# Row maxima of an attention kernel: four a unit as a + relu(b - a), single banks, and a table of paired slots

## The chip, the cores and the metric

The kernel runs on one core of a Trainium2 chip. The metric is device time of one execution in microseconds (us); the median of three runs before the change is 5821.26 us (5820.58 to 5821.32). Engine names are those of the profile: PE is TensorE's matmuls and PEld its weight loads, DVE is VectorE, ACT is ScalarE, POOL is GpSimd, SP is the engine from whose queue the DMAs are issued. PSUM, where matmuls write, has eight banks of 512 float32 columns on 128 partitions.

## The reference

Four transformer layers without MLP: A, B, A, B. A is multi-head attention with its own keys and values per head, B has 32 heads of queries and one shared head of keys and values. All is float32; S = 2048 positions, D = 576, H = 32 heads of 18.

```python
def _A_ref(x, wqkv, wo):
    qkv = (x @ wqkv).reshape(B, S, 3, H, Dh).transpose(2, 0, 3, 1, 4)
    q, k, v = qkv[0], qkv[1], qkv[2]
    scores = jnp.einsum("bhqd,bhkd->bhqk", q, k) * (Dh ** -0.5)
    p = _softmax(scores, axis=-1)
    o = jnp.einsum("bhqk,bhkd->bhqd", p, v)
    return o.transpose(0, 2, 1, 3).reshape(B, S, D) @ wo
# _B_ref is the same with k = x @ wk, v = x @ wv shared by all heads
x = A_x
x = x + _A_ref(_layernorm(x), A_wqkv, A_wo)
x = x + _B_ref(_layernorm(x), B_wq, B_wk, B_wv, B_wo)
# and both once more
```

## The kernel before

Queries and keys are projected, split into a high and a low part so that 54 rows (18 dimensions, three products) carry the precision, and stored to DRAM (`qk_d`); per pair of heads they are loaded back into `big`, head 0 on partitions 0 to 63 and head 1 on 64 to 127. The order of all work is written out by hand: the schedule is manual, each engine's instructions stand in the order in which the program makes them, and a tile waits for its buffer's last user.

The attention loop goes over units. A **unit** is one pair of heads (`p`, 16 of them) and one quarter of the queries (`u`, 512 of them); a layer has 64. A unit has

- 32 score matmuls for the **maxima** (`max_mm`, tile `psm`): for each of two heads `a`, four blocks of 128 queries `qc` and four blocks of 512 keys `kb`, queries on the partitions. DVE takes the maximum of each row of keys (`reduce_max`). `max_final` reduces the four key blocks of each query block to one negated maximum; POOL splits it into two parts, `max_store` transposes it and sends it to DRAM, `max_rows` loads it as two more rows of the query operand. The maxima of a unit are made `LEAD` steps (a step is four exponentials) ahead of its exponentials;
- 32 score matmuls for the **exponentials** (`exp_mm`, tile `pse`): keys on the partitions, 512 queries, with the two rows of the negated maximum in the product; ACT takes `exp` into a tile `pt` of the pool with 15 buffers;
- the **values** (`pv_block`): the `pt` tiles times the values, with a column of ones for the sum, accumulated in the one bank `oacc`: four tiles at a time on four column groups. `pv_cols` issues them as a run of so many columns, 4096 a unit. At the unit's end ACT copies `oacc` out (`oc`), and POOL and DMAs do the division.

A score matmul uses half of PE's rows (54 to 64 of 128), head 0 the upper, head 1 the lower half, so two of different heads can run side by side. The loop goes through `ORDERS`, eleven phases a unit: five of two maxima and three exponentials, five of four and three, one of two and two; after each phase a run of 384 columns of values (256 after the last), two phases behind. In `max_mm` two maxima share a tile of two banks (`mtile2`), and one `reduce_max` of 1024 elements does both.

PSUM before: two tiles of two banks for maxima (tag `m`), three single ones for exponentials (tag `e`), and `oacc`. The tags also serve the projections (`project`, `project_v`, `out_w`), which run between the loops with matmuls of all 128 rows; the first `2 * LEAD` pairs of maxima of a layer are woven between the last projections (`woven`, `beat`, `max_pair`).

```python
for phase in range(11 * 4 * NPAIR):
    k = phase % 11
    run_todo(LEAD + exps // 4)
    for kind, n in ORDERS[2 if k == 10 else k % 2]:
        ...
    exps += 2 if k == 10 else 3
    if phase >= 2:
        pv_cols(256 if k == 10 else 384)
```

## Time and profile before

| | |
|---|---|
| runs | 5821.32, 5821.26, 5820.58 us |
| profiled execution: span, first to last instruction | 5815.8 us; what lies around it is not in the profile (the runs' median is 5.5 us longer) |
| PE busy | 5782.9 us (99%), granted clock 0.998 |
| DVE busy | 5174.9 us (89%), of it 4773.0 in 4096 reductions of 1024 |
| ACT busy | 4604.8 us (79%), of it 4314.2 in 8192 exponentials |
| POOL busy | 1722.0 us (30%) |
| HBM | 45 GB/s over the span |

A group's row gives line, engine, operation, output and input tiles, shapes and count, then the busy time in us and the mean duration of one in ns, then the engine's idle time just before them and what ended it. Neighbouring operations of an engine overlap at their ends, so the distance from start to start is shorter than the duration. A row of the timeline gives start and length in us of a stretch of equal instructions, with their count; matmul rows of neighbouring stretches overlap. A row of a stretch (`A:B`) gives its length, then the busy time and count of PE, PEld, DVE, ACT and POOL, the granted clock, the share of the DMA engines and GB/s.

### The profile page before, as it was taken

To read this page: it belongs to the slowest core of one execution; us is meant where nothing else is said; L and a number is where in the kernel's file an instruction comes from. 1 tells how busy PE (TensorE), PEld (TensorE's weight loads), DVE (VectorE), ACT (ScalarE), POOL (GpSimd) and SP (SyncE) were. 2 spreads that over 40 slices of the span, in tenths; PEclk is the share of its full clock that TensorE was granted. 3 is DMA by queue.
4 is the path that set the end of the run, shared out by engine and by line. 5 is a ranking of instruction groups with operands and counts; after the bars stand their busy time and mean duration, and the time that the engine had idled before them with its cause. 6 is when DMAs were issued, how large, how long until landed. Compare 5 with 4: busy or idle time off the path is not lost.

```text
span 5815.8 us, 132694 instructions
## 1 busy us (share of the span) xinstructions
PE 5782.9 (99%) x53756; PEld 2904.4 (50%) x53756; DVE 5174.9 (89%) x5333; ACT 4604.8 (79%) x8872; POOL 1722.0 (30%) x2210
## 2 busy tenths in 40 slices
PE   8999999999999999999999999999999999999999
PEld 7644444444844444444685444444448444444446
DVE  4699999998699999999647999999976999999995
ACT  2488888888378888888625888888882888888885
POOL 2142323233233232323311323232342332323232
PEclk9999999999999999999999999999999999999999
DMA  5311111110320000001242111111114100000002
GB/s 194 111 42 35 32 35 32 35 32 21 126 65 23 23 20 22 20 23 23 59 167 87 44 35 31 35 31 35 29 32 129 51 22 23 22 23 19 23 14 77
DMA packets 250305, 276.40 MB, mean 48 GB/s; under 512 B 131732, under 2 KB 171924, under 8 KB 239972
## 3 DMA queue, kind: packets, MB, share of 16 engines
q1 hardware_dynamic: 249692, 267.92, 16.6%
q8 instruction: 422, 6.91, 0.5%
q14 instruction: 191, 1.56, 0.1%
HBM read 151.24 MB, written 112.56 MB: 45 GB/s over the span
## 4 chain that ended last, share of the span: by engine, by line
PE 97%; DVE 1%; POOL 0%; ACT 0%; DMA 0%; issue 0%; SPq 0%; POOLq 0%; ACTq 0%; DVEq 0%
PE oacc L683 36%; PE psm L509 31%; PE pse L658 17%; PE psn L219 6%; PE psq L377 6%; DVE mx L518 1%; PE ps L211 0%; ACT pt L662 0%; DMA raw<-in_B_wk_dram 0%; DMA raw<-in_A_wqkv_dram 0%; SPq L153 0%; POOL wsm L168 0%; PE oacc L212 0%; DVE big L168 0%; POOL big L168 0%
## 5 line engine op out<-in xcount | busy, mean ns | idle before, releaser
L518 DVE TENSOR_REDUCE mx<-psm 128x2 f32<-128x1024 f32 x4096 | 4773.0, 1217 | 171.9 <-PE psm L509 131.4
L662 ACT ACTIVATE pt<-pse 128x512 f32<-128x512 f32 x8192 | 4314.2, 602 | 543.5 <-PE pse L658 374.0
L658 PE MATMUL pse<-big 64*128 64x512 f32 x8192 | 2448.8, 417 | 3.5 <-ACT evr L388 1.8
L509 PE MATMUL psm<-big 62*128 62x512 f32 x8192 | 2295.4, 453 | 7.0 <-DVE mx L518 6.7
L683 PE MATMUL oacc<-pt,vbuf 128*19 128x384 f32 (+1 forms) x24560 | 1757.5, 385 | 1.9 <-ACT oc L689 1.9
L509 PEld LDWEIGHTS psm<-big 62*128 62x128 f32 x8192 | 926.3, 184 | 1480.9 <-DVE mx L518 926.7
L658 PEld LDWEIGHTS pse<-big 64*128 64x128 f32 x8192 | 1188.4, 185 | 286.1 <-ACT pt L662 193.6
L683 PEld LDWEIGHTS oacc<-pt,vbuf 128*19 128x19 f32 x24560 | 500.8, 97 | 772.9 <-issue 595.2
L141 POOL TENSOR_SCALAR hl<-neg 128x8 fp32r<-128x8 f32 x256 | 50.9, 199 | 2670.5 <-DVE neg L634 2670.5
L706 POOL TENSOR_TENSOR rl<-lt,mone 128x8 f32<-128x8 f32 x256 | 423.7, 1655 | 568.5 <-DMA lt<-os 568.2
L683 PE MATMUL oacc<-pt,vy 128*19 128x256 f32 x8176 | 591.5, 384 | 0.0
L141 POOL TENSOR_SCALAR os<-oc 32x512 f32<-32x512 f32 x512 | 314.6, 614 | 130.5 <-ACT oc L689 88.7
L719 POOL TENSOR_TENSOR os<-os,rb 96x512 f32<-96x512 f32 x256 | 329.5, 1287 | 21.3 <-DMA rb<-r_d 21.3
L697 POOL TENSOR_TENSOR os<-os,oc 96x512 f32<-96x512 f32 x256 | 326.6, 1276 | 21.4
L385 ACT ACTIVATE ev<-psq 128x512 fp32r<-128x512 f32 (+1 forms) x112 | 67.0, 598 | 335.4 <-PE psq L377 225.4
L219 PE MATMUL psn<-wsm,xx 128*128 128x288 f32 x2240 | 313.3, 297 | 0.0
L219 PEld LDWEIGHTS psn<-wsm,xx 128*128 128x128 f32 x2240 | 299.3, 188 | 15.9 <-issue 15.6
L683 PEld LDWEIGHTS oacc<-pt,vy 128*19 128x19 f32 x8176 | 176.8, 98 | 249.4 <-issue 200.3
L391 DVE TENSOR_TENSOR ev<-psq,ev 128x512 fp32r<-128x512 f32 (+1 forms) x84 | 58.0, 691 | 217.9 <-ACT ev L385 202.6
L377 PE MATMUL psq<-yx,big 128*128 128x512 f32 (+2 forms) x812 | 201.7, 399 | 7.7 <-DVE ev L391 4.8
L377 PE MATMUL psq<-xx,big 128*128 128x512 f32 (+1 forms) x784 | 201.0, 401 | 0.0
L689 ACT ACTIVATE oc<-oacc 128x512 f32<-128x512 f32 x256 | 157.7, 616 | 28.9 <-PE oacc L683 28.9
(70 smaller groups left out, 1372.3 us busy)
## 6 DMA issues: line engine op xcount, KB each, us to landing
big<-qk_d SPq DMA_DIRECT2D x180, 432.0 KB
qk_d<-ev SPq DMA_DIRECT2D x96, 512.0 KB
qk_d<-ev SPq DMA_DIRECT2D x120, 256.0 KB
rb<-r_d SPq DMA_DIRECT2D x512, 36.0 KB
o_d<-os SPq DMA_DIRECT2D x512, 36.0 KB
m_d<-tr SPq DMA_DIRECT2D x1024, 2.0 KB
o<-o_d SPq DMA_DIRECT2D x64, 256.0 KB
big<-m_d SPq DMA_DIRECT2D x512, 4.0 KB
```

The costliest lines, as they stand in the source:

```text
L141: eng.tensor_scalar(dst, src, 1.0, 0.0, op0=OP.mult, op1=OP.add)
L219: nc.tensor.matmul(ps, lhs[:, xc, :], wsm[:, wc, h * 288:(h + 1) * 288], start=i == 0, stop=i == len(TERMS) - 1)
L377: nc.tensor.matmul(ps[:n].rearrange("p (u t) -> p u t", u=2)[:, us], w[:, wc, :n], xts[T][:, us, xc, :], start=(xc, wc) == TERMS[0], stop= ...
L509: nc.tensor.matmul(ps[:, slot], q[b:b + KM, c0:c0 + P], k[b:b + KM, kb * 512:(kb + 1) * 512], start=True, stop=True)
L518: nc.vector.reduce_max(mxs[p, u][:, r0:r1 + 1:r1 - r0], ps, axis=AX.X)
L658: nc.tensor.matmul(e, k[r:r + KE, kc * P:(kc + 1) * P], q[r:r + KE, u * 512:(u + 1) * 512], start=True, stop=True)
L662: nc.scalar.activation(pt, e, AF.Exp, scale=SCALE)
L683: nc.tensor.matmul(oacc[j:j + DH + 1, cs], v_of(kc)[:, 2 * p + a if is_a else 0, :], pts[p, u, i][:, cs], start=kc < 2 and c0 == 0, stop=k ...
L689: nc.scalar.activation(oc, oacc, AF.Copy)
L697: nc.gpsimd.tensor_tensor(t[:96], t[:96], oc[:96], op=OP.add)
L706: nc.gpsimd.tensor_tensor(rl, lts.pop((p, u)), mone, op=OP.pow)
L719: nc.gpsimd.tensor_tensor(t[:96], t[:96], rb[:96], op=OP.mult)
```

## The change

1. **Maxima in pairs of key blocks.** For each head, two of the four query blocks of a unit have their first two key blocks done another way (four in all a unit, two per head): a matmul with the difference of the two key blocks (`d`, tile `psd`) gives b - a, ACT writes relu(b - a) to a tile `r`, and later the matmul of block 0 (`t`) gives a, and one DVE operation adds `r` and takes the maximum over the row: max(a, b) = a + relu(b - a). The other 24 maxima of a unit (`m`) have one `reduce_max` of 512 each. The first three units of a layer (`FIRST_SHARED`) have plain maxima only. The fused DVE operation is built as two instructions, the operation and a read of its accumulator.
2. **Key differences.** `key_diff` makes them while keys are projected (ACT keeps block 0's result, DVE subtracts, POOL splits), stores them to `kd_d`; `load_kd` loads them per pair of heads into the spare buffer `xx[:, 0]`, two DMAs each.
3. **The order.** `UNIT` replaces `ORDERS`: 32 slots a unit, each with one matmul of head 0 and one of head 1 (e exponential, m, d, t maxima), and twelve numbers that issue runs of values, 896 columns behind (`LAG`) instead of two phases. Units without maxima use `LAST`: eight times two slots of exponentials and 512 columns.
4. **Banks.** Three single tiles for maxima (`m` and `t`), four for exponentials and `d`, and `oacc`. The projections that used both banks of a double tile take one of each tag and are drained in halves.
5. **Lead.** `LEAD` is 16 steps instead of 14: 32 pairs of maxima ahead of the loop instead of 28.

In the built program ACT has 8871 activations before and 9875 after and 644 and 1950 separate waits; DVE 4352 and 6496 reductions, 384 and 460 two-input operations, and 976 fused ones with as many accumulator reads after; POOL gets 24 operations more, SP's queue 92 DMAs more. There is one load of ACT's table in both.

```diff
-LEAD = 14
+LEAD = 16
...
+UNIT = """ee md 384 me me em 512 dm md em 320 me ee em 192 em me 384 et ee mm 384 me ee em 384 dm me em 384
+          em me 256 me te ee 256 em em 384 et te me 256"""
+LAST = "ee ee 512 " * 8
+LAG = 896
...
+def max_ops(kinds):
+    pairs = kinds.count("d")
+    rest = [(qc, kb) for qc in range(4) for kb in range(4) if qc >= pairs or kb > 1]
+    seen, ops = {"d": 0, "t": 0}, []
+    for k in kinds:
+        if k == "m":
+            ops.append((k, *rest.pop(0)))
+        else:
+            ops.append((k, seen[k], 0))
+            seen[k] += 1
...
+FIRST_SHARED = 3
...
-    def mtile2(name):
-        return psum.tile([P, 2, 512], F32, tag="m", bufs=2, name=name)
-
     def mtile(name):
-        return mtile2(name)[:, 0]
+        return psum.tile([P, 512], F32, tag="m", bufs=3, name=name)
 
     def etile(name):
-        return psum.tile([P, 512], F32, tag="e", bufs=3, name=name)
+        return psum.tile([P, 512], F32, tag="e", bufs=4, name=name)
...
-        ps = mtile2("psn")
         for h in range(2):
-            natural(ot, h, ps[:, h])
-        xc = xo[:, c, :].rearrange("p (h n) -> p h n", h=2)
-        nc.vector.tensor_tensor(xc, ps[:, :, :288], xc, op=OP.add)
+            ps = natural(ot, h, (etile if h else mtile)("psn"))
+            xc = xo[:, c, h * 288:(h + 1) * 288]
+            nc.vector.tensor_tensor(xc, ps, xc, op=OP.add)
...
+        def key_diff(T, t, ps, r0, r1):
+
+            if T == 0:
+                k0s[t] = ptile("k0")
+                nc.scalar.activation(k0s[t][r0:r1], ps[r0:r1], AF.Copy)
+                return
+            kd, lo, hi = k0s.pop(t), ptile("kl"), ptile("kh", dt=F32R)
+            nc.vector.tensor_tensor(kd[r0:r1], ps[r0:r1], kd[r0:r1], op=OP.subtract)
+            copy(nc.gpsimd, hi[r0:r1], kd[r0:r1])
+            hi_f = hi.bitcast(F32)[r0:r1]
+            nc.gpsimd.tensor_tensor(lo[r0:r1], kd[r0:r1], hi_f, op=OP.subtract)
...
+            if kind == "d":
+                ps = etile("psd")
+                nc.tensor.matmul(ps, q[b:b + 3 * DH, c0:c0 + P], kds[p % 2 if is_a else 0][b:b + 3 * DH],
+                                 start=True, stop=True)
+                r = ptile("r")
+                diffs[a].append(r)
+                nc.scalar.activation(r, ps, AF.Relu)
+            else:
+                ps = tile("psm")
+                nc.tensor.matmul(ps, q[b:b + KM, c0:c0 + P], k[b:b + KM, kb * 512:(kb + 1) * 512],
+                                 start=True, stop=True)
+                if kind == "t":
+                    r = diffs[a].pop(0)
+                    nc.vector.tensor_tensor_reduce(out=r, in0=ps, in1=r, scale=1.0, scalar=-3.0e38, op0=OP.add,
+                                                   op1=OP.max, accum_out=mx[:, r0:r0 + 1])
+                else:
+                    nc.vector.reduce_max(mx[:, r0:r0 + 1], ps, axis=AX.X)
...
-                    woven(max_pair, 10, 5)
+                    woven(max_pair, 12, 4)
...
+            if is_a or p == 0:
+                at(max(LEAD + 32 * (p - 2) + 20, LEAD + 1 + p), load_kd, p)
...
+        late, n_e = LAG, 0
+        for w in range(4 * NPAIR):
+            p, u = divmod(w, 4)
+            more_m = m_done[0] < 4 * ns
+            e_next = [0, 0]
+            for kinds, cols in UNIT if more_m else LAST:
+                run_todo(LEAD + STEPS * w + sum(e_next) // 4)
+                for a in range(2):
+                    if kinds[a] == "e":
+                        n = e_next[a]
+                        e_next[a] += 1
+                        exp_mm(p, u, n // 2 * 4 + 2 * a + n % 2, mtile if not more_m and n_e % 7 % 2 else etile)
+                        n_e += 1
+                    else:
+                        max_mm(a, mtile)
+                skip = min(late, cols)
+                late -= skip
+                pv_cols(cols - skip)
```

More of the change, by code (lines that the diff above doesn't have):

```diff
@@ L59, with slots @@
 TAIL = 2
-ORDERS = ([("m", 1), ("e", 0), ("m", 1), ("e", 1), ("e", 2)],
-          [("m", 0), ("m", 1), ("e", 1), ("e", 0), ("m", 0), ("m", 1), ("e", 2)],
-          [("m", 1), ("e", 0), ("m", 1), ("e", 1)])
+UNIT = """ee md 384 me me em 512 dm md em 320 me ee em 192 em me 384 et ee mm 384 me ee em 384 dm me em 384
+          em me 256 me te ee 256 em em 384 et te me 256"""
+LAST = "ee ee 512 " * 8
+LAG = 896
+def slots(text):
+    out = []
+    for w in text.split():
+        if w.isdigit():
+            out[-1][1] = int(w)
+        else:
+            out.append([w, 0])
+    return out
+UNIT, LAST = slots(UNIT), slots(LAST)
+KINDS = [[w[a] for w, _ in UNIT if w[a] != "e"] for a in range(2)]
+assert sum(n for _, n in UNIT) == 4096 and [len(k) for k in KINDS] == [16, 16]
+def max_ops(kinds):
[8 more added lines that the diff above has]
+            seen[k] += 1
+    assert not rest
+    return ops
+MAX_OPS = [max_ops(k) for k in KINDS]
+PLAIN = [(i // 2 % 4, i // 8 % 2 * 2 + i % 2) for i in range(16)]
+FIRST_SHARED = 3
 @with_exitstack
@@ L114, in tile_kernel @@
     r_d = dram.tile([H, S], F32, name="r_d")
+    kd_d = dram.tile([D, 3, 512], F32, name="kd_d")
     rb = cst.tile([P, 512], F32, name="rb")
+    mxd = [cst.tile([P, 32], F32, name=f"mxd{i}") for i in range(2)]
+    for t in mxd:
+        nc.gpsimd.memset(t, -3.0e38)
+    kds = [xx[:, 0].rearrange("p c t -> p (c t)")[:, 512 * i:512 * i + 512] for i in range(2)]
     sums = [cst.tile([P, 512], F32, name=f"os{i}") for i in range(2)]
@@ L385, in project @@
             nc.scalar.activation(ev[0][:n], ps[:n], AF.Copy)
+            r0, r1 = ((64, P) if t == 4 else (0, P)) if is_a else (96, 96 + DH)
+            if T < 2 and t in (range(4, 9) if is_a else (4,)):
+                key_diff(T, t, ps, r0, r1)
             if filler:
@@ L402, in project, with load_kd @@
                 store(ev_f, 0, P, t * P, t0)
+        def key_diff(T, t, ps, r0, r1):
[8 more added lines that the diff above has]
+            nc.gpsimd.tensor_tensor(lo[r0:r1], kd[r0:r1], hi_f, op=OP.subtract)
+            c0 = t * P + r0 - D if is_a else 0
+            dst = kd_d[c0:c0 + r1 - r0]
+            nc.sync.dma_start(dst[:, 0:2], hi_f[:, None, :].to_broadcast([r1 - r0, 2, 512]))
+            nc.sync.dma_start(dst[:, 2], lo[r0:r1])
+        k0s = {}
+        def load_kd(p):
+            for a in range(2):
+                c = (2 * p + a) * DH if is_a else 0
+                nc.sync.dma_start(kds[p % 2 if is_a else 0].bitcast(F32)[64 * a:64 * a + 3 * DH],
+                                  kd_d[c:c + DH].rearrange("c i t -> (c i) t"))
         def store(ev_f, r0, r1, c0, t0):
@@ L424, in project_v @@
         def project_v(c):
-            ps = mtile2("psn")
-            for h in range(2):
-                natural(xt_of(c), h, ps[:, h])
-            return ps[:, :, :288].rearrange("p h (e d) -> p h e d", d=DH)
+            return [natural(xt_of(c), h, (etile if h else mtile)("psn")).rearrange("p (e d) -> p e d", d=DH)
+                    for h in range(2)]
         def v_dst(c):
@@ L484, in ops @@
             return big[:, q_slot(p)], big[:, k_slot(p)]
-        m_open, m_next, m_done, m_count = [], [0, 0], [0], {}
+        diffs, m_next, m_done, m_count = ([], []), [0, 0], [0], {}
         m_first = [] if is_a else ([(0, i // 2, i % 2) for i in range(8)] + [(1, i // 2, i % 2) for i in range(4)] +
@@ L491, in tile_kernel, with max_mm @@
                                    [(1, i, 2) for i in range(4)] + [(1, i, 3) for i in range(4)])
-        def max_mm(a, slot):
-            i = m_next[a]
-            p, u = divmod(i // 16, 4)
-            if i < len(m_first):
-                u, qc, kb = m_first[i]
-            else:
-                qc, kb = i // 2 % 4, i // 8 % 2 * 2 + i % 2
+        def max_mm(a, tile):
+            n = m_next[a]
+            w, i = divmod(n, 16)
+            shared = w >= FIRST_SHARED
+            kind = "m"
+            if n < len(m_first):
+                w, qc, kb = m_first[n]
+            elif shared:
+                kind, qc, kb = MAX_OPS[a][i]
+            else:
+                qc, kb = PLAIN[i]
+            p, u = divmod(w, 4)
@@ L501, in max_mm @@
             q, k = ops(p)
             if (p, u) not in mxs:
-                mxs[p, u] = pool.tile([P, 32], F32, name="mx")
-            if m_done[0] % 2 == 0:
-                m_open.append((mtile2("psm"), []))
-            ps, rows = m_open[0]
+                mxs[p, u] = mxd[w % 2] if shared else pool.tile([P, 32], F32, name="mx")
+            mx = mxs[p, u]
             b = 64 * a
             c0 = u * 512 + qc * P
-            nc.tensor.matmul(ps[:, slot], q[b:b + KM, c0:c0 + P], k[b:b + KM, kb * 512:(kb + 1) * 512],
-                             start=True, stop=True)
@@ L511, in max_mm @@
-            rows.append((p, u, 16 * a + 4 * qc + kb))
+            r0 = 16 * a + 4 * qc + kb
             m_next[a] += 1
             m_done[0] += 1
-            if m_done[0] % 2 == 0:
-                m_open.pop()
-                (p, u, r0), (p1, u1, r1) = sorted(rows)
-                assert (p, u) == (p1, u1)
-                nc.vector.reduce_max(mxs[p, u][:, r0:r1 + 1:r1 - r0], ps, axis=AX.X)
-                m_count[p, u] = m_count.get((p, u), 0) + 2
-                if m_count[p, u] == 32:
-                    max_final(p, u)
+            if kind == "d":
[15 more added lines that the diff above has]
+                    nc.vector.reduce_max(mx[:, r0:r0 + 1], ps, axis=AX.X)
@@ L523, in max_pair @@
+            m_count[p, u] = m_count.get((p, u), 0) + 1
+            if m_count[p, u] == 32:
+                max_final(p, u)
         def max_pair():
@@ L526, in max_pair @@
             for a in range(2):
-                max_mm(a, a)
+                max_mm(a, etile if a else mtile)
             if not is_a and m_done[0] == 46:
@@ L576, in last_values @@
                     staged.append((c, h, ptile("vst", (P, 16, DH))))
-                    nc.scalar.activation(staged[-1][2], pv[:, h], AF.Copy)
+                    nc.scalar.activation(staged[-1][2], pv[h], AF.Copy)
             vs.append(pool.tile([P, NV], F32, tag="vy", bufs=1, name="vy")
@@ L594, in tile_kernel @@
                 if not is_a and T == 2 and i == 1:
-                    woven(max_pair, 10, 5)
+                    woven(max_pair, 12, 4)
                 elif not is_a and T == 3:
-                    woven(max_pair, *((2, 7), (4, 3), (4, 3))[i])
+                    woven(max_pair, *((3, 4), (4, 3), (4, 3))[i])
                 project(T, t, not is_a and T >= 2)
@@ L618, in tile_kernel @@
                 for c in range(4 * T, 4 * T + 4):
-                    nc.scalar.activation(v_dst(c), project_v(c), AF.Copy)
+                    for h, ps in enumerate(project_v(c)):
+                        nc.scalar.activation(v_dst(c)[:, h], ps, AF.Copy)
         fill = []
@@ L650, in max_rows, with exp_mm @@
                                   m_d[u][:, a].rearrange("j q p -> j (q p)"))
-        def exp_mm(p, u, i, tail):
+        def exp_mm(p, u, i, tile):
             a, kc = (i // 2) % 2, i // 4 * 2 + i % 2
             q, k = ops(p)
-            e = (mtile if tail and i % 2 else etile)("pse")
+            e = tile("pse")
             r = 64 * a
@@ L742, in tile_kernel @@
                 for i in range(4 if is_a else 2):
-                    at(LEAD + 32 * (p - 1) + 1 + 8 * i if p else LEAD + 1 + 4 * i, load_part, p + 1, i)
+                    at(LEAD + 32 * (p - 1) + 1 + 8 * i if p else LEAD + 1 + 3 * i, load_part, p + 1, i)
+            if is_a or p == 0:
+                at(max(LEAD + 32 * (p - 2) + 20, LEAD + 1 + p), load_kd, p)
         for c in range(5):
@@ L768, in tile_kernel @@
         assert not weave["left"]
-        exps = 0
-        for phase in range(11 * 4 * NPAIR):
-            k = phase % 11
-            run_todo(LEAD + exps // 4)
-            for kind, n in ORDERS[2 if k == 10 else k % 2]:
-                if kind == "e":
-                    n += exps
-                    exp_mm(*divmod(n // 4 // STEPS, 4), n % (4 * STEPS), m_done[0] >= 4 * ns)
-                elif m_done[0] < 4 * ns:
-                    max_mm(n ^ k // 2 % 2, m_done[0] % 2 if k % 2 == 0 else n ^ k // 2 % 2)
-            exps += 2 if k == 10 else 3
-            if phase >= 2:
-                pv_cols(256 if k == 10 else 384)
+        late, n_e = LAG, 0
+        for w in range(4 * NPAIR):
+            p, u = divmod(w, 4)
+            more_m = m_done[0] < 4 * ns
+            e_next = [0, 0]
+            for kinds, cols in UNIT if more_m else LAST:
+                run_todo(LEAD + STEPS * w + sum(e_next) // 4)
+                for a in range(2):
+                    if kinds[a] == "e":
[3 more added lines that the diff above has]
+                        n_e += 1
+                    else:
+                        max_mm(a, mtile)
+                skip = min(late, cols)
+                late -= skip
+                pv_cols(cols - skip)
+            assert e_next == [16, 16]
+        assert not diffs[0] and not diffs[1]
         outs = out_proj(layer == 3)
@@ L786, in tile_kernel @@
                 next(outs)
-                pv_cols(256 * (1 + st - ns))
+                pv_cols(LAG - 512 if st == ns else 512)
         tail = [todo.pop(n, []) for n in range(ns + LEAD + L_AT + 1, ns + LEAD + O_AT)]
```

## The prediction

> **What bounds the kernel now.** I read the page first: its span, the busy shares, the granted clock, the chain of waits and the costliest groups.

> ```profile
> span 5815.8 us, 132694 instructions
> ...
> PE 5782.9 (99%) x53756; PEld 2904.4 (50%) x53756; DVE 5174.9 (89%) x5333; ACT 4604.8 (79%) x8872; POOL 1722.0 (30%) x2210
> ...
> PEclk9999999999999999999999999999999999999999
> ...
> PE 97%; DVE 1%; POOL 0%; ACT 0%; DMA 0%; issue 0%; SPq 0%; POOLq 0%; ACTq 0%; DVEq 0%
> ...
> L518 DVE TENSOR_REDUCE mx<-psm 128x2 f32<-128x1024 f32 x4096 | 4773.0, 1217 | 171.9 <-PE psm L509 131.4
> L662 ACT ACTIVATE pt<-pse 128x512 f32<-128x512 f32 x8192 | 4314.2, 602 | 543.5 <-PE pse L658 374.0
> L658 PE MATMUL pse<-big 64*128 64x512 f32 x8192 | 2448.8, 417 | 3.5 <-ACT evr L388 1.8
> ```

> PE is on the chain for 97% at a full clock. But "PE busy" says little about whether it could go faster, so the second view is the four stretches between the layers' ends, and the third one the drain of `oacc`, which comes once a unit (32 exponentials, 32 maxima, 4096 columns of values).

> ```profile
> 1760.00:2840.00 1080.00, 1079.69 (x10709) 480.34 (x10709) 1038.03 (x996) 962.58 (x1846) 340.20 (x414) 1.00 0.10 22
> ```

> ```profile
> L689 ACT ACTIVATE oc<-oacc x5: 615/616/617, 2013.7 to 2091.1; 128x512 f32<-128x512 f32 x5
> ```

> Four units in 2091.1 - 2013.7 = 77.4 us: 19.35 us a unit; 256 of them are 4954 us, 85% of the span. In these stretches DVE is busy for 96% and ACT for 89%. So two engines run near their limit, and the unit is the place to count. The timeline of PE shows its three kinds of stretch:

> ```profile
> 2003.04 0.50 PE L509 MATMUL psm<-big 62*128 62x512 f32 x2
> 2003.38 0.40 PE L658 MATMUL pse<-big 64*128 64x512 f32 x2
> 2003.62 0.39 PE L509 MATMUL psm<-big 62*128 62x512 f32 x2
> 2003.85 0.40 PE L658 MATMUL pse<-big 64*128 64x512 f32 x1
> 2004.17 0.85 PE L683 MATMUL oacc<-pt,vbuf 128*19 128x128 f32 x16
> 2004.95 0.49 PE L509 MATMUL psm<-big 62*128 62x512 f32 x1
> ...
> 2005.86 0.85 PE L683 MATMUL oacc<-pt,vbuf 128*19 128x256 f32 x16
> 2006.64 0.50 PE L509 MATMUL psm<-big 62*128 62x512 f32 x2
> ...
> 2008.56 0.49 PE L509 MATMUL psm<-big 62*128 62x512 f32 x1
> ...
> 2009.22 0.63 PE L683 MATMUL oacc<-pt,vbuf 128*19 128x256 f32 x8
> 2009.78 0.50 PE L509 MATMUL psm<-big 62*128 62x512 f32 x1
> ```

> Two score matmuls on different halves of the rows start together and cost one slot. Seven matmuls (2003.04 to 2004.17) take four slots, 1.13 us: the seventh has no partner. Two slots (2008.56 to 2009.22) take 0.66, so an inner slot is 0.235 and three are 0.90 (2004.95 to 2005.86 shows 0.91). 384 columns of values take 0.78, 256 take 0.56: 0.22 per 128 columns, and 0.12 fixed for each run.

> A unit of before is five odd phases of four slots, five even ones of three, one of two (37 slots for 64 matmuls), ten runs of 384 columns and one of 256: 5x1.13 + 5x0.90 + 0.66 + 10x0.78 + 0.56 = 19.17. The unit's 19.35 leaves 0.18 of waits.

> The other two engines, in the same terms (the distance between starts where the engine has work, not the busy time of one):

> ```profile
> 2012.00 3.49 DVE L518 TENSOR_REDUCE mx<-psm 128x2 f32<-128x1024 f32 x3 [0.20 <-PE psm L509]
> 2015.52 0.19 DVE L634 TENSOR_REDUCE neg<-mx 128x8 f32<-128x32 f32 x1
> 2015.65 2.36 DVE L518 TENSOR_REDUCE mx<-psm 128x2 f32<-128x1024 f32 x2
> 2017.93 0.20 DVE L643 STREAM_TRANSPOSE tr<-hl 128x32 f32<-128x32 f32 x1
> 2018.05 4.69 DVE L518 TENSOR_REDUCE mx<-psm 128x2 f32<-128x1024 f32 x4
> ```

> ```profile
> 2012.22 1.57 ACT L662 ACTIVATE pt<-pse 128x512 f32<-128x512 f32 x3 [0.30 <-PE pse L658]
> 2013.67 0.62 ACT L689 ACTIVATE oc<-oacc 128x512 f32<-128x512 f32 x1
> 2014.15 5.00 ACT L662 ACTIVATE pt<-pse 128x512 f32<-128x512 f32 x9
> ```

> DVE: (2017.93 - 2015.65)/2 = 1.14 a reduction of 1024; the closing reduction and the transpose add 0.13 and 0.12, and 0.11 ahead of the closing one. 16x1.14 + 0.36 = 18.6 of 19.35. ACT: 0.48 each (2012.22 to 2013.67 three, 2013.67 to 2014.15 one); 33 of them 15.84.

> **The change, part by part.** *Slots.* The table has 32 slots, each with one matmul on either half, in eight runs of three and four of two, and twelve runs of values. Scores 8x0.90 + 4x0.66 = 9.84; values 4096 columns x 0.22/128 = 7.04, and 12x0.12 = 1.44. PE's unit becomes 18.32: 0.85 less than 19.17, although one run is added.

> *DVE.* Sixteen reductions of two banks become 24 of one bank and four fused add-and-max with an accumulator read behind each. No row shows a reduction of 512. From 1217 ns at 1024 and 187 at 32 an element costs 1.04 ns, so 1.14 - 0.53 = 0.61. A two-input operation of that size agrees (126.94 to 127.55):

> ```profile
> 126.94 0.69 DVE L391 TENSOR_TENSOR ev<-psq,ev 128x512 fp32r<-128x512 f32 x1 [2.61 <-DMA qk_d<-ev]
> 127.55 0.68 DVE L205 TENSOR_TENSOR xx<-ps,xx 128x512 fp32r<-128x512 f32 x1
> ```

> The accumulator read is in no row; between 0 and the 0.20 of the transpose; I take 0.13, as the smallest reduction takes until the next one starts. The fused operation could also run at half rate (another 0.53 each); I don't take that, as 126.94 has the same operands at full rate. DVE: 24x0.61 + 4x0.74 + 0.36 = 17.96 (18.2 with 0.20 for the read).

> *ACT.* Four Relu more, priced as the exponentials: 37x0.48 = 17.76. [...]

> *New waits.* The fused operation waits for its Relu tile, made at least eleven slots earlier (slots 2, 6, 7, 20 for 14, 26, 30, 31: over 5 us), so DVE and the maxima queued behind it don't feel it. Those tiles come out of the 15 buffers that the exponentials use, so four ACT operations a unit wait for DVE; each stands at least a run behind the fused operation that frees its buffer. Were DVE a run late, ACT, then the values and PE behind them, would be late with it (rival 1).

> *Banks.* Two double banks and three single become three and four. PE waits where a bank is late, and everything behind it in its queue waits too, values included. Summing table and durations run by run, ACT's backlog never passes about two operations with four banks to hold it, and DVE's two with three; yet many margins are 0.05 to 0.25 us, about an inner slot.

> *Sum of a unit.* Loads are then PE 18.32, DVE 17.96, ACT 17.76, where they were 19.17, 18.6, 15.84. Before, 0.18 of waits came on PE with one engine close behind it. With two behind it I take 0.33: 18.65, 0.70 less. No waits at all would be 18.32, and I bound the other end by DVE keeping the idle 0.75 of before on top of 18.2 with every late wait's 0.3: 19.25.

> *What is outside.* 61 units a layer take the new form: 244 x 0.70 = 171 us off. The longer lead puts four more pairs of maxima ahead of the loop (4 x 0.66 = 2.6 a layer) and takes a quarter unit of maxima out of it at the end, where ACT then sets 33x0.48 = 15.8 (0.25 x 3.5 = 0.9 saved). The first unit of a layer has plain maxima only, DVE 32x0.61 + 0.36 = 19.9: 0.6 more. Key differences add 12 tiles in all on ACT, DVE and POOL, 24 operations of POOL (30% busy) and 92 transfers in SP's queue (DMA share 0.10 in the row above), under the projections' matmuls; uncovered, a copy and a two-input operation like these, 12 x 1.9 = 23 us.

> ```profile
> L141 POOL TENSOR_SCALAR os<-oc 32x512 f32<-32x512 f32 x512 | 314.6, 614 | 130.5 <-ACT oc L689 88.7
> ...
> L697 POOL TENSOR_TENSOR os<-os,oc 96x512 f32<-96x512 f32 x256 | 326.6, 1276 | 21.4
> ```

>  Output and value projections drain in halves: 64 more DVE operations under PE's work. I take +5 in all (-10 to +30).

> The profiled execution's span is 5815.8; the runs' median 5821.26 lies 5.5 above it, which I take as what lies around the span: 5821 - 171 + 5 = 5655.

> **The rivals.**
> 1. DVE's fixed cost per instruction decides; slower. Place: DVE, 28 instructions where there were 16. The price is what one takes beyond its elements: 0.08 in 0.61. DVE is back at the 18.6 of before from 0.64/28 = 0.023 more, 0.10 an instruction. The closing reduction speaks for it: it takes 0.13 to the next start for 32 elements (0.033), a fixed 0.10. The 0.61 of 126.94 and the 1.14 speak against. [...] Chance 0.15 (a half-rate fused operation, 4x0.53, would land in the same place).
> [...]
> 2. No wait at all: the unit is PE's 18.32: 5821 - 251 + 5 = 5575. For it: PE waited only 0.18 before. Against: three engines within 3% of each other. Chance 0.15.
> 3. The margins are too thin: PE waits for banks on both sides, 18.9 to 19.3, around 19.1: 5821 - 61 + 5 = 5765. For it the thin margins; against, that a wait on PE lets the others catch up. Chance 0.17.
> 4. It all cancels, 19.35: 5826 or so. Chance 0.03.

> **How the numbers follow.** Forecast (18.45 to 18.9, its own range 5606 to 5716) 0.50, rivals 0.15, 0.15, 0.17, 0.03. The range 5550 to 5830 goes from under rival 2 (rounding of the runs, 0.1 a unit) to rival 4, and leaves out most of rival 1. Faster by over 0.2% (12 us, about what a measurement can tell): 0.50 + 0.15 + 0.17 = 0.82; same 0.03; slower 0.15.

> **What would show it.** `oc` every 18.65 us; a three-slot run 0.90 and a 384-column run 0.78; reductions of 512 starting 0.61 apart, the fused one with its read 0.74; Relu 0.48; DVE and ACT both near 95%, PE still the chain. It would be wrong if DVE is over 98% with PE's weight loads waiting for `mx`, or if ACT waits for late values or `r`.

## The result

The changed kernel takes 5725.72 us (median of four runs, 5719.78 to 5730.9), the kernel before 5820.92 beside it: ratio 0.9837, 95% interval 0.9823 to 0.9851. It is faster by 95 us. The forecast was 5655 with a range of 5550 to 5830: the sign and the place of the gain are right, the size is 71 us too good. The time lies 10 us above the forecast's own 5606 to 5716; the stated range holds it because it was drawn out to the rivals.

The page of the kernel after, in the parts that answer to those shown of before (span, busy time by engine, chain, costliest groups; L738 are the exponentials, L593 the plain reductions, L590 the fused operation, L583 the Relu):

```profile
span 5727.0 us, 136567 instructions
...
PE 5670.4 (99%) x51804; PEld 2876.1 (50%) x51804; DVE 4936.5 (86%) x9505; ACT 4915.4 (86%) x9876; POOL 1744.0 (30%) x2236
...
PE 96%; issue 1%; ACT 1%; POOL 1%; DMA 1%; DVE 1%; SPq 0%; ACTq 0%; POOLq 0%; DVEq 0%
...
L738 ACT ACTIVATE pt<-pse 128x512 f32<-128x512 f32 x8192 | 4202.5, 633 | 122.6 <-PE pse L734 53.2
L593 DVE TENSOR_REDUCE mxd<-psm 128x1 f32<-128x512 f32 x5856 | 3689.7, 682 | 115.9 <-PE psm L586 52.6
...
L590 DVE CUSTOM_DVE_ANT_0 r<-psm,r 128x512 f32<-128x512 f32 x976 | 652.7, 688 | 140.3 <-PE psm L586 118.3
...
L583 ACT ACTIVATE r<-psd 128x512 f32<-128x512 f32 x976 | 581.8, 625 | 0.6 <-PE psd L579 0.6
```

DVE has given up 238 us of busy time (5174.9 before), ACT has gained 311, and in this mean over the whole span the two are now level. ACT's idle time ahead of the exponentials fell from 543.5 us to 122.6. The stretch of the four units, and the one that the prediction read for the loads:

```profile
L765 ACT ACTIVATE oc<-oacc x5: 597/597/598, 2010.0 to 2085.1; 128x512 f32<-128x512 f32 x5
```

```profile
1760.00:2840.00 1080.00, 1075.30 (x10489) 496.57 (x10488) 975.43 (x1873) 1039.16 (x2084) 350.43 (x423) 1.00 0.11 26
```

(2085.1 - 2010.0)/4 = 18.775 us a unit against 19.35. In the stretch ACT went from 89% to 96% and DVE from 96% to 90% (its last part is the end of a layer, where the loop has no maxima). From 1800 to 2400 us, all inside the loop, ACT is busy for 589.8 of 600 us and DVE for 566.1; before it was 534.2 and 582.9. Busy time counts whole durations, which overlap (an exponential of after lasts 0.63 us, and the next one starts 0.48 behind it), so it overstates the loads.

To part the loops from the rest, take the copies `oc` of each layer; each row has a layer's 64, the time of its first and of its last one. Before, and then after:

```profile
L689 ACT ACTIVATE oc<-oacc x64: 598/616/617, 250.4 to 1475.9; 128x512 f32<-128x512 f32 x64
L689 ACT ACTIVATE oc<-oacc x64: 599/616/617, 1645.7 to 2866.0; 128x512 f32<-128x512 f32 x64
L689 ACT ACTIVATE oc<-oacc x64: 598/616/617, 3144.1 to 4369.0; 128x512 f32<-128x512 f32 x64
L689 ACT ACTIVATE oc<-oacc x64: 599/617/617, 4540.2 to 5760.1; 128x512 f32<-128x512 f32 x64
```

```profile
L765 ACT ACTIVATE oc<-oacc x64: 597/597/898, 254.7 to 1445.9; 128x512 f32<-128x512 f32 x64
L765 ACT ACTIVATE oc<-oacc x64: 597/598/952, 1634.4 to 2823.1; 128x512 f32<-128x512 f32 x64
L765 ACT ACTIVATE oc<-oacc x64: 597/597/1005, 3108.6 to 4296.1; 128x512 f32<-128x512 f32 x64
L765 ACT ACTIVATE oc<-oacc x64: 597/598/899, 4483.7 to 5671.3; 128x512 f32<-128x512 f32 x64
```

From first to last, the layers took 1225.5, 1220.3, 1224.9, 1219.9 us and take 1191.2, 1188.7, 1187.5, 1187.6: together 135.6 less. Ahead of the first `oc` and between the layers it was 250.4, 169.8, 278.1, 171.2 and is 254.7, 188.5, 285.5, 187.6: together 46.8 more. Less 135.6 and plus 46.8 is the 88.8 by which the spans differ. So the loop gave most of what was forecast, and a third of it went again at the layers' edges.

### The profile page after: what moved, and what is told of

Its sections match the earlier page's. It is cut to its first block, busy times and chain, and to the rows that moved or that the text cites. A ratio compares the mean times of both kernels' runs of the same rounds, so it can differ in the third digit from the quotient of the medians.

```text
span 5727.0 us, 136567 instructions
## 1 busy us (share of the span) xinstructions
PE 5670.4 (99%) x51804; PEld 2876.1 (50%) x51804; DVE 4936.5 (86%) x9505; ACT 4915.4 (86%) x9876; POOL 1744.0 (30%) x2236
## 4 chain that ended last, share of the span: by engine, by line
PE 96%; issue 1%; ACT 1%; POOL 1%; DMA 1%; DVE 1%; SPq 0%; ACTq 0%; POOLq 0%; DVEq 0%
PE oacc L759 37%; PE pse L734 22%; PE psm L586 20%; PE psn L257 6%; PE psq L414 6%; PE psd L579 4%; ACT pt L738 1%; PE ps L249 0%; POOL ev L429 0%; DVE mx L593 0%; DMA raw<-in_B_wk_dram 0%; DMA raw<-in_A_wqkv_dram 0%; DMA big<-qk_d 0%; SPq L191 0%; PE oacc L250 0%
## 5 line engine op out<-in xcount | busy, mean ns | idle before, releaser
L738 ACT ACTIVATE pt<-pse 128x512 f32<-128x512 f32 x8192 | 4202.5, 633 | 122.6 <-PE pse L734 53.2
L593 DVE TENSOR_REDUCE mxd<-psm 128x1 f32<-128x512 f32 x5856 | 3689.7, 682 | 115.9 <-PE psm L586 52.6
L586 PE MATMUL psm<-big 62*128 62x512 f32 x7216 | 2629.2, 450 | 10.3 <-DMA big<-qk_d 6.4
L759 PE MATMUL oacc<-pt,vbuf 128*19 128x384 f32 (+5 forms) x23584 | 1789.0, 396 | 20.7 <-ACT oc L765 17.3
L586 PEld LDWEIGHTS psm<-big 62*128 62x128 f32 x7216 | 1188.9, 184 | 644.6 <-DVE mxd L593 255.8
L590 DVE CUSTOM_DVE_ANT_0 r<-psm,r 128x512 f32<-128x512 f32 x976 | 652.7, 688 | 140.3 <-PE psm L586 118.3
L759 PE MATMUL oacc<-pt,vy 128*19 128x128 f32 (+2 forms) x7200 | 593.4, 414 | 1.2
L583 ACT ACTIVATE r<-psd 128x512 f32<-128x512 f32 x976 | 581.8, 625 | 0.6 <-PE psd L579 0.6
L579 PE MATMUL psd<-xx,big 54*128 54x512 f32 x976 | 402.9, 452 | 0.0
L773 POOL TENSOR_TENSOR os<-os,oc 96x512 f32<-96x512 f32 x256 | 327.6, 1280 | 21.3
L593 DVE TENSOR_REDUCE mx<-psm 128x1 f32<-128x512 f32 x384 | 244.1, 685 | 56.6 <-PE psm L586 49.7
L579 PEld LDWEIGHTS psd<-xx,big 54*128 54x128 f32 x976 | 162.0, 184 | 258.5 <-ACT pt L738 207.2
```

The lines of the kernel that those rows point to most:

```text
L579: nc.tensor.matmul(ps, q[b:b + 3 * DH, c0:c0 + P], kds[p % 2 if is_a else 0][b:b + 3 * DH], start=True, stop=True)
L583: nc.scalar.activation(r, ps, AF.Relu)
L586: nc.tensor.matmul(ps, q[b:b + KM, c0:c0 + P], k[b:b + KM, kb * 512:(kb + 1) * 512], start=True, stop=True)
L590: nc.vector.tensor_tensor_reduce(out=r, in0=ps, in1=r, scale=1.0, scalar=-3.0e38, op0=OP.add, op1=OP.max, accum_out=mx[:, r0:r0 + 1])
L593: nc.vector.reduce_max(mx[:, r0:r0 + 1], ps, axis=AX.X)
L738: nc.scalar.activation(pt, e, AF.Exp, scale=SCALE)
```

## The experiments

Each table keeps the 64 score matmuls and 4096 columns of values of a unit; all runs compute the whole result. "Unit" is the distance of `oc` as above.

### e1: the same table without sharing

```diff
-FIRST_SHARED = 3
+FIRST_SHARED = 64
```

All 32 maxima of a unit are plain reductions in the slots that `d`, `t` and `m` had; the key differences are still made.

> The changed kernel with plain maxima in every unit (32 reductions of 512, no Relu, no difference matmul); table, single banks and lead as changed. If the sharing is what frees VectorE: its unit is 32 x 0.60 + 0.36 = 19.6 us and the unit goes from 18.77 to about 19.9, the whole to 5726 + 244 x 1.13 = 6000 us, slower than the kernel before. If the pairing of the slots alone made the gain, the unit stays at 18.8 and the whole within 5720 to 5740.

Measured 6352.2 us, ratio 1.0915 (1.0899 to 1.0931), unit 21.35. Much slower than either expectation had it. DVE's load for 32 reductions, 32x0.61 + 0.36 = 19.9, doesn't explain 21.35, so the order of the slots is in it too; e10 and e12 take that apart.

### e2: pairing of slots alone

The table of after without sharing, and the banks of before (two double ones, three single), each double one filled by two maxima, mostly from two slots, and reduced at once.

```diff
-FIRST_SHARED = 3
+FIRST_SHARED = 64
...
-        return psum.tile([P, 512], F32, tag="m", bufs=3, name=name)
+        return mtile2(name)[:, 0]
...
-        return psum.tile([P, 512], F32, tag="e", bufs=4, name=name)
+        return psum.tile([P, 512], F32, tag="e", bufs=3, name=name)
...
+                if len(rows) == 1:
+                    return
```

> The table of 32 paired slots and the lead as changed, but the maxima as before: two double banks, one reduction of 1024 for two maxima, three banks for exponentials, no sharing. TensorE's floor is the 18.2 to 18.3 of the changed kernel, VectorE's load the 18.5 of before. If both halves of the change are needed: unit about 19.0 to 19.1, 5726 + 244 x 0.28 = 5795 us. If the pairing does it all: 18.8, about 5720 to 5730. If the pairing does nothing because VectorE was the real bound: 19.35, about 5860.

Measured 7194.02 us, ratio 1.2362 (1.2343 to 1.238), unit 24.6, far above all three cases of the expectation. The timeline of DVE shows it standing between nearly all reductions:

```profile
2004.11 2.36 DVE L610 TENSOR_REDUCE mx<-psm 128x2 f32<-128x1024 f32 x2 [0.94 <-PE pse L751]
2006.86 1.23 DVE L610 TENSOR_REDUCE mx<-psm 128x2 f32<-128x1024 f32 x1 [0.39 <-PE psm L596]
2008.26 1.23 DVE L610 TENSOR_REDUCE mx<-psm 128x2 f32<-128x1024 f32 x1 [0.17 <-PE pse L751]
```

In this table a maximum's slot partner is mostly an exponential, so a double bank's second half often comes a run later; until then nothing can be reduced, and PE, which keeps to the program's order, stands for the other bank (from 2000 to 2400 us its weight loads wait 87.4 us for DVE's `mx`, 114 times). 37 slots to 32 are worth nothing with these banks and this order. I had summed loads and overlooked that. The timeline agrees with this; that it is the whole cause isn't shown.

### e3: the weaving of before

Only the last projections of a B layer differ: the maxima woven between them go back to the spacing of before.

```diff
-                    woven(max_pair, 12, 4)
+                    woven(max_pair, 10, 5)
...
-                    woven(max_pair, *((3, 4), (4, 3), (4, 3))[i])
+                    woven(max_pair, *((2, 7), (4, 3), (4, 3))[i])
```

> Only the weaving of the first maxima into the projections of the B layers is put back to a pair after every five matmuls (10 pairs, then 2, 4, 4 as before). If the denser weaving is what makes TensorE wait there and drop to half clock: the B layers lose the 15 us each that they gained in that stage, about 5726 - 30 = 5696 us, and the half-clock stretches there go. If the cause is that the maxima of head 1 share the four banks of the exponentials with the transposes, it stays within 10 us of 5726.

Measured 5705.93 us, ratio 0.9804 (0.9788 to 0.982): 20 us better than after and the fastest kernel of all. The unit is the same; the four layers of e3:

```profile
L765 ACT ACTIVATE oc<-oacc x64: 597/597/1005, 255.2 to 1443.0; 128x512 f32<-128x512 f32 x64
L765 ACT ACTIVATE oc<-oacc x64: 597/598/952, 1624.6 to 2813.3; 128x512 f32<-128x512 f32 x64
L765 ACT ACTIVATE oc<-oacc x64: 597/597/1005, 3098.9 to 4286.4; 128x512 f32<-128x512 f32 x64
L765 ACT ACTIVATE oc<-oacc x64: 597/598/1005, 4464.8 to 5651.5; 128x512 f32<-128x512 f32 x64
```

The gaps ahead of the two B layers are 181.6 and 178.4 (169.8 and 171.2 before, 188.5 and 187.6 after); the one ahead of the second A layer, which the edit doesn't touch, is 285.6 as in after. The tighter weaving is 16 of the 35 us that the two B layers' edges lost; the other 19 stay. That is the first case of the expectation in kind, two thirds of it in size; the last section has the clock.

### e4, e9, e11: three shared maxima, and two

```diff
# e4: against after; head 0's second pair plain
- ... dm me em 384 em me 256 me te ee 256 em em 384 et te me 256
+ ... mm me em 384 em me 256 me te ee 256 em em 384 et me me 256
# e9: three, no run with more than three maxima (weaving as e3)
+ ... me me em 384 em mm 256 me te ee 256 em em 384 et me me 256
# e11: two, one of each head (against e9)
- ... dm md em 320 me ee em 192 ... et me me 256
+ ... dm me em 320 me em em 192 ... em me me 256
```

> Three shared maxima a unit where there are four (head 0's second one is plain): ScalarE 36 operations instead of 37 (17.2 us of work instead of 17.7), VectorE 29 instead of 28 (17.7 instead of 17.1). If ScalarE, busy for 98% of the changed unit, sets its remaining 0.5 us of waits: unit about 18.5 to 18.6, 5726 - 50 = 5676 us. If VectorE's banks set them: unit about 19.0, 5780 us. If the waits are those of the pairs and runs themselves: 18.75 to 18.8 as it is.

> Three shared maxima a unit as in the earlier run of that kind (unit 19.57), but an exponential and a plain maximum change places between the eighth and the ninth run, so that no run has more than three operations for the three maxima's banks (there the eighth had four, and ScalarE stood still for 1.05 us at that place). Weaving as before, so compare with 5706 us. If a run that asks for more banks than there are is what costs: that stop goes, ScalarE is what is left with 36 x 0.477 + 1.1 to 1.3 = 18.3 to 18.5, whole 5706 - 244 x 0.35 = about 5620 us (5595 to 5660). If VectorE's larger share (29 operations) costs, not the place: unit 19.3 or more, 5830 us or more.

> Two shared maxima a unit (one a head), arranged so that no run has more than three maxima or four exponentials; weaving as before. ScalarE 35 x 0.477 + 1.1 = 17.8, VectorE 30 x 0.60 + 0.36 = 18.4, TensorE's floor 18.2. If ScalarE's load set the changed unit and VectorE now takes over: unit 18.5 to 18.7, whole 5640 to 5690 us. If VectorE with 30 operations and three banks needs more than its sum: unit 19 or more, 5760 us or more.

Measured: e4 5911.7 us, ratio 1.0158 (1.0143 to 1.0173), unit 19.55; e9 5839.22, 1.0032 (1.0019 to 1.0044), unit 19.3; e11 5901.68, 1.0142 (1.0126 to 1.0157), unit 19.6. None gains from the operations that it spares ACT. ACT's timeline of e4 and of e9:

```profile
2002.90 1.09 ACT L738 ACTIVATE pt<-pse 128x512 f32<-128x512 f32 x2 [0.97 <-PE psm L586]
```

```profile
2014.96 5.50 ACT L738 ACTIVATE pt<-pse 128x512 f32<-128x512 f32 x11 [1.16 <-PE pse L734]
```

ACT has less work there and loses more than that by standing about 1 us once a unit. In e4 it stands behind the run `mm me em`, four maxima for three banks; e9 took that run away and got 0.25 of the unit back, and ACT then stands behind `em mm`, a run with a single exponential. What PE's weight loads waited for in front of these two stalls (1999.5 to 2003.2 us of e4, then 2012.5 to 2015 of e9; a row gives the total in us, the times and the longest):

```profile
PEld psm L586 <- DVE mxd L593: 1.0, 3, 0.6
```

```profile
PEld psm L586 <- DVE mxd L593: 0.8, 2, 0.4
```

PE is held up by banks that DVE hasn't drained: the two slots of `em mm` take 1.24 us (2012.60 to 2013.84) where 0.66 is usual, and ACT runs out of exponentials meanwhile. So an operation given back to DVE cost more here than ACT saved, and e9 and e11 came out as the second case of their expectations. DVE isn't full over a whole unit (568.3 of 600 us busy in e9 from 1800 to 2400 us, 566.1 after); it is late in places. Whether another order with two or three shared maxima avoids this isn't shown, and the stall of e11 wasn't followed.

### e5: a bank moved to the maxima

```diff
# against e1
-        return psum.tile([P, 512], F32, tag="m", bufs=3, name=name)
+        return psum.tile([P, 512], F32, tag="m", bufs=4, name=name)
...
-        return psum.tile([P, 512], F32, tag="e", bufs=4, name=name)
+        return psum.tile([P, 512], F32, tag="e", bufs=3, name=name)
```

> The kernel without sharing (32 plain reductions of 512, unit 21.37 us) with four banks for maxima and three for exponentials instead of three and four. In the runs so far unit time over operations that use the maxima's banks is the same: 18.77/28, 19.57/29, 21.37/32, all 0.67 us, or 2.0 us a bank with three of them. If that turnaround of a bank sets the unit: four banks make it 32 x 0.50, so VectorE's own 32 x 0.60 + 0.36 = 19.6 decides, unit about 19.8, whole about 5980 us. If VectorE takes 0.67 an operation in any case: it stays at 21.3, whole 6350 us. If the exponentials with three banks become the limit: above 21.4, over 6360 us.

Measured 6462.07 us, ratio 1.1101 (1.1084 to 1.1118), unit 21.7: another 110 us slower than e1. This is the third case of the expectation: in this table the bank is worth more to the exponentials than to the maxima. Three, four and `oacc` make eight banks, as many as before has; four and four beside `oacc` weren't tried.

### e6, e7: double banks with tables made for them

A slot has two maxima, one of each head, and they fill one double bank, which is so complete within a slot (no sharing, no key differences, weaving of before).

```diff
# e6, against e2; e7 has the second line
+UNIT = "mm ee mm 384 ee mm ee 384 mm ee 256 " * 4
+UNIT = "mm ee mm ee 512 " * 8
```

> Pairing alone, with a table made for it: no sharing and no key differences; double banks for maxima with one reduction of 1024 (as before), both matmuls of a double bank in one slot; three banks for exponentials; slots alternate mm and ee in twelve runs of 3, 3, 2 slots with 384, 384, 256 columns; weaving as before. TensorE's floor 18.2, VectorE 16 x 1.13 + 0.36 = 18.45. If the bank's turnaround is what cost the pairing alone its gain in the other table (unit 24.6): a double bank is filled and drained at once here, VectorE decides, unit 18.6 to 18.9, whole 5690 to 5760 us, about the changed kernel's. If maxima cannot be had in this time without the sharing: unit 19.3 or more, 5850 us or more.

> The same with eight runs of four slots and 512 columns: TensorE's floor falls to 8 x (1.13 + 0.12) + 6.83 = 16.8, VectorE's 18.45 stays. If VectorE decides: unit 18.5 to 18.7, 0.1 to 0.2 under the twelve runs, whole 5670 to 5720 us. If the long runs of values (1.0 us) leave VectorE without work with two double banks: unit 19 or more, 5780 us or more.

Measured: e6 6742.43 us, ratio 1.158 (1.1563 to 1.1597), unit 23.1; e7 6870.73, 1.1801 (1.1781 to 1.182), unit 23.6. Better than e2, still far behind before, whose eleven phases of `ORDERS` reach 19.35 with the same banks. DVE's timeline of e6 waits once a run:

```profile
2003.58 4.72 DVE L607 TENSOR_REDUCE mx<-psm 128x2 f32<-128x1024 f32 x4 [0.63 <-PE psm L593]
2008.99 3.60 DVE L607 TENSOR_REDUCE mx<-psm 128x2 f32<-128x1024 f32 x3 [0.70 <-PE psm L593]
```

Both have the lag of 896 columns, which in these tables, unlike that of after, puts a unit's end into the middle of a run: from 2000 to 2400 us PE stands for the copy `oc` once a unit, 1.3 us each in e6 (22.4 in 17 times) and 0.7 in e7 (12.1 in 17). e10 and e12 below show what that costs there; with double banks another lag wasn't tried. So these are not the best tables of their kind, and that no order exists in which pairing pays with double banks isn't shown.

### e8: five shared maxima

One more `d` and `t`, on head 1 (weaving as e3).

```diff
-          em me 256 me te ee 256 em em 384 et te me 256"""
+          ed me 256 me te ee 256 em et 384 et te me 256"""
```

> Five shared maxima a unit instead of four (head 1 gets a third one, its difference in the ninth run, its sum in the eleventh), weaving as before (compare with 5706 us). If the turnaround of the maxima's three banks sets the unit: 27 x 0.67 = 18.1, then TensorE's floor of 18.2 and ScalarE's 38 x 0.477 = 18.1 decide, unit about 18.5, whole about 5640 us. If ScalarE sets it: 19.1, whole about 5790 us.

Measured 5821.41 us, ratio 1.0 (0.9991 to 1.0009). Unit and loads of e8:

```profile
L765 ACT ACTIVATE oc<-oacc x5: 597/597/597, 2015.3 to 2092.2; 128x512 f32<-128x512 f32 x5
```

```profile
1760.00:2840.00 1080.00, 1078.05 (x10342) 471.45 (x10334) 954.95 (x1880) 1066.06 (x2133) 340.63 (x414) 1.00 0.09 22
```

(2092.2 - 2015.3)/4 = 19.23: 0.45 more than after for one Relu more, which costs 0.48, though DVE has one operation less (88% where after has 90%). 38x0.48 = 18.24 leaves 0.99 of waits, and after's 37x0.48 = 17.76 leaves 1.02. This points to ACT as what sets the unit of after, as the case with 19.1 had it; ACT is busy for 593.1 of 600 us from 1800 to 2400 us. The added `d` and `t` also change the order of the table, so this one run doesn't prove it. In e9 the step the other way costs about as much (19.3): of the counts tried, four is the best.

### e10 and e12: no sharing, in a table made for it

No maximum shared, at most three maxima a run, 32 slots, three single banks and four, weaving as e3. e12 differs from e10 by the lag alone, so that a unit ends at the end of a run.

```diff
# e10, against e9
+UNIT = "me em me 384 em me em 384 me em 256 " * 4
-FIRST_SHARED = 3
+FIRST_SHARED = 64
# e12, against e10
-LAG = 896
+LAG = 1024
```

> No sharing, with a table that never asks for more than three maxima or three exponentials in a run (12 runs, single banks, three and four), weaving as before. The earlier run without sharing kept a table made for sharing, with up to five maxima in a run (unit 21.37). If bursts over the banks cost most of that: VectorE is what is left, 32 x 0.598 + 0.36 = 19.5, unit 19.6 to 19.9, whole 5900 to 5980 us; that is what the sharing is worth. If the 0.67 us an operation is a property of the banks: 21.3, 6320 us.

> This is the kernel of e10_none_spread (no maximum shared, 32 slots, at most three maxima a run) with the lag of the values set from 896 to 1024 columns, so that a unit's last values are issued at the end of a run and the first scores of the next run lie between them and the next unit's values. Theory 1: the 1.33 us gap that VectorE has once a unit in e10_none_spread is PE's wait for ScalarE's copy of the output (oc), which had come into the middle of a run. Then the unit falls by about 1.3 us from 21.1 to about 19.8, VectorE is back to back with 32 reductions of 0.597 and the tail, and the whole is about 6259 - 244 x 1.3 = 5940 us (5900 to 5980). Sharing, against a table laid as well without it, is then worth about 1.0 us a unit. Theory 2: the gap is made by the order of the slots in the table, whatever the lag: the unit stays at 21.0 to 21.2 and the whole between 6230 and 6270 us.

Measured: e10 6259.19 us, ratio 1.0755 (1.074 to 1.0769), unit 21.1; e12 5944.37, ratio 1.021 (1.0193 to 1.0227), unit 19.8. The unit of e10 looks like the second case of its expectation, a price of the banks, but e12 shows that it is neither case. In e10, DVE's timeline has one hole a unit, and in the waits of 2000 to 2400 us PE and its weight loads stand for the copy `oc`:

```profile
2010.84 2.44 DVE L592 TENSOR_REDUCE mx<-psm 128x1 f32<-128x512 f32 x4
2014.52 14.76 DVE L592 TENSOR_REDUCE mx<-psm 128x1 f32<-128x512 f32 x24 [1.24 <-PE pse L733]
```

```profile
PEld oacc L758 <- ACT oc L764: 26.4, 19, 1.4
PE oacc L758 <- ACT oc L764: 21.1, 19, 1.1
```

In e12 the scores of the next run lie between a unit's last values and the next unit's first, and the copy is over by then. The hole is gone; loads, then DVE's timeline of e12:

```profile
1760.00:2840.00 1080.00, 1080.00 (x10468) 453.44 (x10464) 1077.15 (x1855) 944.47 (x1800) 331.85 (x409) 1.00 0.09 22
```

```profile
2002.56 16.01 DVE L592 TENSOR_REDUCE mx<-psm 128x1 f32<-128x512 f32 x26
2018.61 0.19 DVE L709 TENSOR_REDUCE neg<-mx 128x8 f32<-128x32 f32 x1
```

The fall, 314.8 us, is 244 x 1.29, as the first theory had it. e12 is bound by DVE at almost 100%: (16.01 - 0.68)/25 = 0.613 from start to start, and 32 of these alone are 19.6 of the 19.8. Against it the kernel e3, which shares four and has the same weaving, is 238 us faster: between these two tables, sharing is worth 1.0 us a unit.

## Why the prediction was right, and where it was off

**Where the gain is: right.** It was to come from the unit, with PE still the chain, ACT and DVE close behind. e12 and e3 split it: paired slots and single banks without sharing, in the best table tried, are slower than before by 0.45 a unit (19.8 against 19.35), since 32 reductions of 0.61 take DVE longer than 16 of 1.14; sharing then takes 1.02 off. So in the tables tried the pairing paid only with sharing; e2, e6 and e7 didn't get it to pay with double banks. Sharing without the pairing, in the order of before, wasn't tried.

**The prices: right, one too high.** Reductions, fused operations and value runs of after:

```profile
2013.70 0.84 PE L759 MATMUL oacc<-pt,vbuf 128*19 128x384 f32 x8
2014.47 0.50 PE L734 MATMUL pse<-big 64*128 64x512 f32 x1
...
2015.40 0.85 PE L759 MATMUL oacc<-pt,vbuf 128*19 128x128 f32 x16
```

A reduction takes (3.68 - 0.68)/5 = 0.60 (forecast 0.61), the fused one with its read 2015.77 - 2015.15 = 0.62 (forecast 0.74: the next reduction starts together with the read, which costs nothing), 384 columns of values 0.77 (0.78), a run of three slots here 0.93 (0.90), a Relu 0.48 (0.48). With these prices DVE's load is 24x0.60 + 4x0.62 + 0.36 = 17.2 and not 17.96: of the two engines that the forecast saw close behind PE, only ACT is. The 19.25 that bounds the unit's other end has 0.3 for late waits in it, which no run shows: ACT's separate waits take 17 ns (median) in both traces, and its operations start 0.48 apart in both where it has work.

**Rival 1 falls.** DVE would be back at the 18.6 of before from 0.023 more an instruction, some 0.63 a reduction; the rows have 0.60. A fixed cost is there all the same, in the small: two of 0.60 against one of 1.14.

**The unit: right mechanism, 0.12 short.** 18.775 lies in the forecast's own 18.45 to 18.9. The term that was mis-sized is the waits, 0.33 on PE's floor of 18.32; they are 0.46. Times 244 this is 30 us. They lie in the runs of scores: from 2000 to 2400 us a run of three slots takes 0.95 on average (shortest 0.89) and one of two 0.69 (0.66). The forecast set the waits between two engines near their limit and didn't say which closes; e8 points to ACT, whose load it had right (37x0.48 = 17.76). Two rows of the waits of 2000 to 2400 us before, then three after, show PE's weight loads turn from DVE to ACT:

```profile
PEld psm L509 <- DVE mx L518: 75.3, 166, 0.6
...
PEld pse L658 <- ACT pt L662: 15.7, 82, 0.2
```

```profile
PEld pse L734 <- ACT pt L738: 58.8, 159, 0.6
...
PEld psm L586 <- DVE mxd L593: 22.4, 54, 0.5
PEld psd L579 <- ACT pt L738: 17.8, 21, 0.8
```

For each of the 20.7 and 21.3 units in these 400 us, that is 3.6 us for DVE before and 1.1 after, 0.8 for ACT before and 3.6 after; with the smaller rows of after (22.3 us more for DVE, 14.0 for ACT) it is 2.1 for DVE and 4.3 for ACT. These are idle times of the weight loads, which run beside PE's matmuls (in these 400 us of after PE is busy for 400.0 and PEld for 181.1), and not time that PE lost. Rival 2 (no wait, 18.32) and rival 3 (19.1) bracket what came. For the four-shared table the margins were thin, as rival 3 has it, but held; e4, e9 and e11 show how near the edge they are: each changes a few slots and stands 0.5 to 0.8 a unit higher.

**Outside the units: the step that failed.** "I take +5 in all (-10 to +30)" came out at 46.8, over its own upper end. By the spans the forecast was 166 us less and 88.8 came, 77 too good (71 by the medians, which differ by 95): 42 of it is here, 30 in the units, and 5 in the last units of the layers, which have no maxima. The terms that the prediction priced here add up to 4 x (2.6 + 0.6 - 0.9) = 9, so the +5 is not even their sum. It had the longer lead right in kind and took it at PE's slots (2.6 a layer); it costed the weaving of those maxima at nothing more, and by e3 that is 16 us at the two B layers. The first unit of each layer, forecast 0.6 longer, takes 1.7 to 3.9 us longer from its first exponentials to its `oc` (12 us over the four layers). The rest, some 19 us, isn't assigned: the longer lead accounts for 10 by the prediction's own price, and what the key differences cost by themselves wasn't tried. A cost that runs through all of these was put at nothing: the prediction took PE at a full clock everywhere. The last section has what the trace shows of that.

## What to carry to other kernels

Where several engines stand as close as here (18.32, 17.76 and 17.2 us a unit), the sum of loads gives the floor, and the order decides whether it is reached (18.775 came): check run by run that no run asks for more banks of a kind than there are (not enough by itself, as e9 shows), that each engine gets work in every run, and that a unit's last piece ends where other work covers the copy behind it (1.3 us a unit in e10). Moving work from DVE to ACT paid here up to four Relu a unit (18.775) and not with a fifth (19.23, e8): count one operation beyond to see where this is. And price the edges of the loops by the work that is woven there, not by the slots alone (46.8 us came where +5 was taken), and look at the granted clock there (0.87 in two first units of after).

## What the runs showed of the hardware

The granted clock fell where PE had only stuttered. The first unit of a layer (first exponentials to first `oc`), the second and the third layer of before, and then of after:

```profile
1622.00:1646.00 24.00, 23.36 (x211) 10.35 (x209) 22.57 (x22) 20.94 (x41) 1.68 (x3) 1.00 0.41 119
...
3119.00:3144.00 25.00, 24.07 (x209) 10.68 (x210) 22.70 (x22) 20.74 (x40) 1.69 (x3) 0.93 0.46 128
```

```profile
1607.00:1634.00 27.00, 25.41 (x195) 10.70 (x194) 23.17 (x40) 20.23 (x40) 2.03 (x5) 0.87 0.34 98
...
3082.00:3108.00 26.00, 24.79 (x195) 10.44 (x194) 21.74 (x37) 19.77 (x39) 1.89 (x5) 0.87 0.46 134
```

The windows are set around that unit, to a whole us: it takes some 24 at a full clock and 25 at 0.93 in the kernel before, 26 and 27 at 0.87 after. At half clock a mean of 0.93 over 25 us is 3.5 us, one of 0.87 over 26 or 27 is 6.8 to 7.0. The timeline of PE ahead of one such stretch and the stretch itself:

```profile
1607.09 0.50 PE L734 MATMUL pse<-big 64*128 64x512 f32 x1
1608.39 0.50 PE L734 MATMUL pse<-big 64*128 64x512 f32 x1 [0.79 <-ACT evr L428]
...
1609.70 0.50 PE L586 MATMUL psm<-big 62*128 62x512 f32 x1 [0.34 <-DVE mx L593]
...
1610.30 1.99 PE L586 MATMUL psm<-big 62*128 62x512 f32 x3
```

```profile
1611.00:1618.00 7.00, 6.89 (x30) 2.71 (x32) 5.50 (x10) 2.79 (x6) 0.00 (x0) 0.53 0.33 97
```

Two waits of 0.79 and 0.34 us are the longest ones there, and behind them PE runs at about half clock (0.53 granted) for 7 us.

The trace's record of the clock has two values only, full and half (1.0 and 0.5), and half clock in stretches of 3.4, 6.8 or 10.2 us. They add up to 27 us before, 96 after and 55 in e3 (mean clock over the span 0.998, 0.992 and 0.995). In the first units of the four layers they are 0, 0, 3.4 and 3.4 us before and 6.8, 6.8, 6.8 and 10.2 after; ahead of the first `oc` and between the layers, those units included, 17 us before, 68 after and 41 in e3. What such a stretch costs can be estimated from a pattern of PE that repeats, four matmuls of a projection and two maxima: 2.73 us from start to start at half clock (1551.83 to 1554.56 us of after), 1.54 at full clock (1560.60 to 1562.14), so some 0.43 of its length. By this estimate the clock is about 10 of the 12 us that the first units lost, 22 of the 46.8 us of all edges, and 12 of the 16 us that e3 won back. No run holds the clock fixed, so how much of the loss it causes, and how much of it only follows the stutter, stays open, and so does what lets it fall.
